# One v tile as a third fp32 load on Scalar's queue, and lambda as one row spread by a PE product

## The chip, the cores and the metric

The kernel runs on one core of a Trainium2 chip. The time is device time in microseconds (us). The kernel before takes 226.63 us (three runs, 226.57 to 226.72).

The profile is one execution. Its engines are PE (TensorE matmul), PEld (TensorE weight loads), DVE (VectorE), ACT (ScalarE), POOL (GpSimd) and SP (SyncE). Its span is about 2 us shorter than the time of the run (224.5 against 226.6). Times inside an execution count from the start of the span. `L238` in a profile line is line 238 of that kernel; the change adds lines, so L238 of before is L247 of after.

## The reference, cut to what matters

A decayed linear attention over 4 batches and 8 heads of 768 positions by 64, and behind it a gated feed-forward layer (512 to 1536 to 512) on its output.

```python
pos = np.arange(block); rel = pos[:, None] - pos[None, :]
Dmask = np.where(rel >= 0, lam[:, None, None] ** rel[None, :, :], 0.0)
...
for b in range(nb):
    intra = np.einsum('bhic,bhjc->bhij', qb, kb) * Dmask[None]
    intra = np.einsum('bhij,bhjd->bhid', intra, vb)
    inter = np.einsum('bhid,bhde->bhie', qb * lam_pow[None], kv_state)
    out[:, :, sl] = intra + inter
    kv_state = lam_block[...] * kv_state + np.einsum('bhsd,bhse->bhde', kb_dec, vb)
...
gate = 1.0 / (1.0 + np.exp(-(x @ w_gate)))
return (gate * (x @ w_val) @ w_out)
```

The kernel takes blocks of 128 positions, six of them. `lam` is eight numbers; each partition needs all of them, for the decay of q (`lamq`) and for the mask.

## The kernel before

Each engine is given its instructions in the order in which the program is written, and where it matters here the traces show it keeping to that order (in h below, PE starts on a k that landed at 7.03 us only at 7.34, behind the transposes of q). The feed-forward products of block n fill PE while the attention of the next block is prepared; block 0 has nothing to hide behind, so its loads and its attention are the head of the kernel.

Three queues of loads feed the head: GpSimd's (`software_dynamic` in part 3 of the page), whose loads go from fp32 to bf16 on the way; Scalar's and Sync's (`hardware_dynamic` there) bring two q tiles as fp32, which are cast on an engine.

```python
lam_bc = const.tile([128, H], FP32, tag="lam_bc")
nc.sync.dma_start(out=lam_bc, in_=lam.partition_broadcast(128))     # 128 x 32 bytes
WG = const.tile([128, NMT, DFF], BF16, tag="WG")                    # and WV, WO
...
q01 = [const.tile([128, H, D], FP32, tag=f"q{b}f", name=f"q{b}f") for b in range(2)]
nc.scalar.dma_start(out=q01[0], in_=q[0, :, 0:C, :].rearrange("h s d -> s h d"))
nc.sync.dma_start(out=q01[1], in_=q[1, :, 0:C, :].rearrange("h s d -> s h d"))
Q[0] = qkv.tile([128, B, H, D], BF16, tag="qb", name="qb")
...
load(0, "k", 0, 2)        # GpSimd's queue, fp32 in DRAM to bf16 in SBUF
load(0, "k", 2, 4)
load(0, "q", 2, 3)
load(0, "q", 3, 4)
load(0, "v", 0, 1)
load(0, "v", 1, 2)
load(0, "v", 2, 3)
load_w(WG, wg_r, 0, GW // 2)
...
idle(10)                  # products of zeros, which keep PE busy
nc.vector.tensor_copy(Q[0][:, 0], q01[0])
piece_tq0([0])            # PE transposes of q, then QS on DVE
make_mask(0)
idle(1)
piece_tq0([1])
piece_tk0(0)              # PE transposes of k ("tk"), then KS copies on ACT
make_mask(1)
idle(1)
piece_s(0, [0])           # scores "sp" = KS x QS
piece_m(0, 0)             # masked scores "MT" on DVE
piece_s(0, [1])
piece_m(0, 1, (0,))
piece_tk0(1)
...
piece_a0(0)               # "op" = MT x v, copied to XT
piece_a0(1)
idle(2)
piece_a0(2, (nc.scalar.copy, nc.scalar.copy))
g0 = psum()
mm_part(g0, WG, 0, 0, 0, 3 * C)      # the first feed-forward product, "gp"
```

A tile pool hands out SBUF one tile after the other (here each started on a multiple of 32 bytes). The pool `const` comes first, `qkv` (the bf16 tiles of q, k and v) right behind it. The built program lists where each tile starts, in bytes within a partition:

```
                before                 after
lam_bc          16512                  16512
lam1                -                  16544   (32 bytes)
WG              16544                  16576
q0f, q1f        53408, 55456           53440, 55488
v0f                 -                  57536   (2048 bytes)
ones                -                  512 bytes, behind zero
first qkv tile  68352 = 534 x 128      70944 = 554 x 128 + 32
```

A load by GpSimd of q, k or v writes each head of a position as one run of 64 bf16 numbers, so 128 bytes (in the trace these loads are packets of 128 bytes). In before each such run starts on a multiple of 128 bytes.

## Time and profile before

| | before |
|---|---|
| time, median (range, runs) | 226.63 us (226.57 to 226.72, 3) |
| span of the profiled run | 224.5 us |
| PE busy | 217.8 us, 97% |
| first k landed | 7.53 us |
| first feed-forward product (gp) starts | 14.51 us |

The page of before, part 1 (busy us, share of the span, instructions) and part 4 (shares of the chain that ended last):

```profile
PE 217.8 (97%) x1746; PEld 114.7 (51%) x1746; DVE 105.8 (47%) x192; ACT 79.8 (36%) x151; POOL 79.2 (35%) x78
...
PE 94%; DMA 3%; ACT 1%; issue 1%; DVE 0%; POOLq 0%
```

PE bounds the kernel; the 3% of DMA on the chain is one load, the first k. The chain of waits of before in the first 15.6 us (start, duration, what):

```profile
1.26 6.26 DMA kb<-in_k_dram
...
7.57 0.41 PE tk L238 x4
...
8.01 1.08 ACT KS L267 x2
...
9.90 0.59 ACT KS L267
...
11.18 0.44 DVE QS L256
...
13.78 0.29 PE op L313 x3
...
14.51 1.14 PE gp L434 x6
```

The first k load is issued at 1.26 us and lands at 7.53; the engines then pass the work on with almost no slack until the first feed-forward product. A microsecond more on k's landing should be a microsecond on the whole.

The view of loads of before in the first 20 us (destination and source, issuing queue, number, KB each, median us from issue to landing):

```profile
kb<-in_k_dram POOLq DMA_DIRECT2D x2, 256.0 KB, 6.5
vb<-in_v_dram POOLq DMA_DIRECT2D x4, 128.0 KB, 6.2
q0f<-in_q_dram ACTq DMA_DIRECT2D x1, 256.0 KB, 4.2
lam_bc<-in_lam_dram SPq DMA_DIRECT2D x1, 4.0 KB, 3.1
```

Lambda's 4 KB take 3.1 us, where the 256 KB of the first q take 4.2.

### The profile page before, as it was taken

How to read it: one execution, taken by the hardware profiler on the slowest of the kernel's cores; microseconds unless marked ns; L12 is line 12 of the kernel's file. 1: busy time of each engine (PE TensorE's matmuls, PEld its weight loads, DVE VectorE, ACT ScalarE, POOL GpSimd, SP SyncE). 2: the span in 40 equal slices, each digit the busy share in tenths (PEclk: the TensorE clock that was granted, in tenths of full speed). 3: DMA queues.
4: the chain of work that ended last, by engine and by line, in shares of the span. 5: the costliest groups of instructions: out<-in, count | busy, mean ns of one | idle time of the engine just before them, and what ended most of it. 6: DMA issues, size and time to landing. Idle time of an engine off the chain costs nothing.

```text
span 224.5 us, 4262 instructions
## 1 busy us (share of the span) xinstructions
PE 217.8 (97%) x1746; PEld 114.7 (51%) x1746; DVE 105.8 (47%) x192; ACT 79.8 (36%) x151; POOL 79.2 (35%) x78
## 2 busy tenths in 40 slices
PE   7689999999999999999999999999999999999994
PEld 2454455888854454444445444446444445444443
DVE  7797747595521713336732445742335840333300
ACT  5564334435422234333225333115333225333221
POOL 8996698983592008930006940000000000000000
PEclk9999999999999999999999999999999999999999
DMA  6999999999999992999021999021930012100022
GB/s 109 155 169 193 191 176 155 163 183 168 157 162 159 225 236 86 210 157 101 1 96 55 231 151 128 0 96 47 168 70 0 0 52 91 47 3 0 0 93 95
DMA packets 106419, 25.70 MB, mean 114 GB/s; under 512 B 97056, under 2 KB 103456, under 8 KB 106400
## 3 DMA queue, kind: packets, MB, share of 16 engines
q0 software_dynamic: 81792, 13.90, 81.6%
q1 hardware_dynamic: 23568, 11.28, 20.4%
q10 hardware_dynamic: 1040, 0.26, 0.5%
q8 instruction: 13, 0.21, 0.4%
q14 instruction: 6, 0.05, 0.1%
HBM read 28.32 MB, written 6.29 MB: 154 GB/s over the span
## 4 chain that ended last, share of the span: by engine, by line
PE 94%; DMA 3%; ACT 1%; issue 1%; DVE 0%; POOLq 0%
PE po L483 27%; PE gp L420 21%; PE vp L426 21%; PE gp L455 5%; PE gp L434 5%; PE vp L461 5%; PE sp L300 3%; PE op L313 3%; DMA kb<-in_k_dram 3%; PE op L325 1%; PE po L472 1%; PE cp L404 1%; ACT KS L267 1%; PE tk L238 1%; ACT XT L352 0%
## 5 line engine op out<-in xcount | busy, mean ns | idle before, releaser
L429 DVE TENSOR_TENSOR ht<-sg,vp 128x512 bf16<-128x512 bf16 x54 | 37.1, 687 | 64.2 <-PE vp L426 64.0
L483 PE MATMUL po<-WO,ht 128*128 128x512 bf16 x276 | 62.0, 379 | 0.0
L420 PE MATMUL gp<-XT,WG 128*128 128x512 bf16 x216 | 55.5, 379 | 0.0
L426 PE MATMUL vp<-XT,WV 128*128 128x512 bf16 x216 | 55.4, 379 | 0.0
L423 ACT ACTIVATE sg<-gp 128x512 bf16<-128x512 f32 x54 | 32.2, 597 | 59.0 <-PE gp L420 59.0
L483 PEld LDWEIGHTS <-ht 128*128 128x128 bf16 x276 | 26.3, 98 | 31.0
L426 PEld LDWEIGHTS <-WV 128*128 128x128 bf16 x216 | 21.2, 98 | 25.5
L420 PEld LDWEIGHTS <-WG 128*128 128x128 bf16 x216 | 20.8, 98 | 24.7
L486 ACT COPY ob<-po 128x512 f32<-128x512 f32 x23 | 13.5, 586 | 52.2 <-PE po L483 50.4
L204 DVE TENSOR_TENSOR MT<-sp,mask 128x512 bf16<-128x512 f32 x40 | 25.1, 682 | 9.1 <-PE sp L300 9.1
L382 POOL TENSOR_TENSOR sd<-Sb,dec 128x512 f32<-128x512 bf16 x8 | 8.1, 1037 | 41.2 <-DVE Sb L411 41.1
L455 PE MATMUL gp<-XT,WG 128*128 128x256 bf16 x96 | 14.4, 273 | 0.0
L461 PE MATMUL vp<-XT,WV 128*128 128x256 bf16 x96 | 14.4, 273 | 0.0
L465 DVE TENSOR_TENSOR ht<-sg,vp 128x256 bf16<-128x256 bf16 x24 | 10.0, 420 | 8.6 <-PE vp L461 8.6
L458 ACT ACTIVATE sg<-gp 128x256 bf16<-128x256 f32 x24 | 9.2, 384 | 13.0 <-PE gp L455 11.8
L91 POOL DMA_DIRECT2D vb<-in_v_dram x10 | 12.7, 1278 | 1.0 <-DMA WG<-in_moe_w_gate_dram 0.6
L373 POOL TENSOR_TENSOR kd<-kb,kds 128x1024 bf16<-128x1024 bf16 x6 | 11.3, 1904 | 4.7 <-PE vp L461 4.7
L411 DVE TENSOR_TENSOR Sb<-cp,sd 128x512 bf16<-128x512 f32 x8 | 5.2, 686 | 15.5 <-PE cp L404 15.5
L340 ACT CAST XT<-op 128x512 bf16<-128x512 f32 x19 | 9.9, 598 | 2.1 <-PE op L313 2.0
L455 PEld LDWEIGHTS <-WG 128*128 128x128 bf16 x96 | 9.2, 98 | 1.7 <-issue 0.2
L461 PEld LDWEIGHTS <-WV 128*128 128x128 bf16 x96 | 9.4, 98 | 1.1
L77 POOL DMA_DIRECT2D qb<-in_q_dram x8 | 9.4, 1182 | 0.0
(79 smaller groups left out, 162.1 us busy)
## 6 DMA issues: line engine op xcount, KB each, us to landing
out_dram<-ob SPq DMA_DIRECT2D x21, 256.0 KB, 2.0
kb<-in_k_dram POOLq DMA_DIRECT2D x10, 256.0 KB, 8.4
qb<-in_q_dram POOLq DMA_DIRECT2D x8, 256.0 KB, 8.1
vb<-in_v_dram POOLq DMA_DIRECT2D x4, 512.0 KB, 13.7
WO<-in_moe_w_out_dram POOLq DMA_DIRECT2D x3, 512.0 KB, 8.7
WV<-in_moe_w_val_dram POOLq DMA_DIRECT2D x5, 256.0 KB, 8.8
WG<-in_moe_w_gate_dram POOLq DMA_DIRECT2D x4, 256.0 KB, 8.6
qb<-in_q_dram POOLq DMA_DIRECT2D x6, 128.0 KB, 8.3
```

The source lines that it names most:

```text
L91: nc.gpsimd.dma_start(out=lst[n][:, b0:b1], in_=src[b0:b1, :, sl, :].rearrange("b h s d -> s (b h) d"))
L204: nc.vector.tensor_tensor(out=out.rearrange("p (e x) c -> p e x c", e=2), in0=x.rearrange("p (e x) c -> p e x c", e=2), in1=mask.rearrange ...
L373: nc.gpsimd.tensor_tensor(out=KD[n][:, e], in0=K[n][:, e], in1=kds[:, e::2].unsqueeze(1).unsqueeze(3).to_broadcast([128, B, HP, D]), op=AL ...
L420: nc.tensor.matmul(gp, lhsT=WG[:, mt, fs], rhs=x[:, mt, :], start=(mt == 0), stop=(mt == NMT - 1))
L423: nc.scalar.activation(sg, gp, AF.Sigmoid)
L426: nc.tensor.matmul(vp, lhsT=WV[:, mt, fs], rhs=x[:, mt, :], start=(mt == 0), stop=(mt == NMT - 1))
L429: nc.vector.tensor_mul(HT[n, ft], sg, vp)
L434: nc.tensor.matmul(ps[:, lo:hi], lhsT=W[:, mt, ft * 128:(ft + 1) * 128], rhs=x[:, mt, lo:hi], start=(mt == 0), stop=(mt == NMT - 1))
L455: nc.tensor.matmul(gp[:, cs], lhsT=WG[:, mt, fs], rhs=x[:, mt, cs], start=(mt == 0), stop=(mt == NMT - 1))
L461: nc.tensor.matmul(vp[:, cs], lhsT=WV[:, mt, fs], rhs=x[:, mt, cs], start=(mt == 0), stop=(mt == NMT - 1))
L483: nc.tensor.matmul(po, lhsT=HT[n, ft][:, tt * 128:(tt + 1) * 128], rhs=WO[:, ft, :], start=(ft == 0), stop=(ft == NFT - 1))
L486: nc.scalar.copy(ob, po)
```

## The change

Two halves. The v half: batch 0's v no longer comes as a load on GpSimd's queue but as a third fp32 load on Scalar's hardware queue, with a cast on ACT; every GpSimd load behind it moves up one place. The lambda half: instead of 128 descriptors of 32 bytes, one row of lambda is loaded and PE spreads it (a row of ones times the row of lambda). The ten idle products are split in four, before that product, and six.

```diff
     lam_bc = const.tile([128, H], FP32, tag="lam_bc")
-    nc.sync.dma_start(out=lam_bc, in_=lam.partition_broadcast(128))
+    lam1 = const.tile([1, H], FP32, tag="lam1")
+    nc.sync.dma_start(out=lam1, in_=lam.partition_broadcast(1))
 ...
     nc.sync.dma_start(out=q01[1], in_=q[1, :, 0:C, :].rearrange("h s d -> s h d"))
+    v0f = const.tile([128, H, D], FP32, tag="v0f")
+    nc.scalar.dma_start(out=v0f, in_=v[0, :, 0:C, :].rearrange("h s d -> s h d"))
 ...
+    V[0] = qkv.tile([128, B, H, D], BF16, tag="vb", name="vb")
 ...
+    ones = const.tile([1, 128], FP32, tag="ones")
+    nc.vector.memset(ones, 1.0)
 ...
-    load(0, "v", 0, 1)
     load(0, "v", 1, 2)
 ...
+    idle(4)
+    lamp = ps_at.tile([128, H], FP32, name="lamp", tag="ps")
+    nc.tensor.matmul(lamp, lhsT=ones, rhs=lam1, start=True, stop=True)
     lnl = const.tile([128, H], FP32, tag="lnl")
-    nc.scalar.activation(lnl, lam_bc, AF.Ln)
+    nc.scalar.activation(lnl, lamp, AF.Ln)
 ...
-        nc.scalar.activation(lnp[us, :], lam_bc[us, u::2], AF.Ln)
+        nc.scalar.activation(lnp[us, :], lamp[us, u::2], AF.Ln)
+    nc.scalar.copy(lam_bc, lamp)
 ...
-        parts = 2 if n == 0 and tt < 2 else 1
+        parts = 2 if n == 0 and tt < 1 else 1
 ...
-    idle(10)
+    idle(6)
 ...
     piece_m(0, 1, (0,))
+    nc.scalar.copy(V[0][:, 0], v0f)
     piece_tk0(1)
```

## The prediction

> **What bounds the kernel.** The page gives PE 217.8 of 224.5 us (97%); the chain of waits is 94% PE. From 16.67 us PE runs nearly without a break (timeline); only the first 16 us can give time. There the chain is: first k load issued 1.26, landed 7.53 us -> transposes -> two KS copies on ACT (8.01-9.08) -> sp -> third KS (9.90) -> fourth -> QS on DVE (11.18) -> sp -> five mask products back to back on DVE (11.85-14.92) -> op of batch 2 (13.78, released by its mask product, not by v) -> XT -> gp (14.51).
>
> **What the change removes.** One GpSimd load. These land 0.85 us apart (10.04, 10.89, 11.75, 12.58, 13.45 us), so each load behind v0 should land about 0.85 us sooner. Few are waited for on the chain: v0 is not (op starts 12.31, v0 landed 11.75); v1 (12.58) costs 0.06 us, hidden by the mask products; v2 and v3 nothing. The only later chain stall on a load is at the block-1 k transposes, 32.29 us: 0.16 us. Gain: about 0.15 us.
>
> **What it moves.** v0 as fp32 (1024 packets of 256 B) goes behind q0 on Scalar's queue. [...] while q1's packets run (4.3-5.3 us), k gets 6 to 79 packets per 0.1 us, afterwards 120. v0 needs some 1.0 us at q's rate. Against that, lambda's broadcast goes: its 128 packets of 32 B drag from 1.7 to 3.5 us, and meanwhile q0 gets 42 packets per 0.1 us, afterwards 75. Estimate: three fp32 loads at 1000 packets per us from 2.1 us end at 5.2 us, where two end at 5.3 now. So the first k should land at 7.5 us, give or take 0.3; this goes one to one into the time.
>
> **What it adds.** A PE product ([...]the idle products keep their number, 10), a lambda copy on ACT (0.2 us, like its neighbours), the v0 cast on ACT (0.62 us, like q1's). The cast falls between the second KS and the third, a gap of 0.82 us: free, if v0 has landed by 9.1; I expect 6. The PE product delays the first q transposes by perhaps 0.3 us (5.79 -> 6.1); they have slack until k lands. The store split once less is neutral.
>
> **Prediction.** 226.63 - 0.15 +- 0.3 (k): 226.5 us, 226.0 to 227.2. Faster by over 2%: 1%; within 2%: 98%; slower: 1%.
>
> **What the profile would show.** First k landing 7.2-7.9 us; lambda near 2.5 instead of 3.82; v0 5.5-6.5; v1 about 11.75; first WG about 13.3; third KS at 9.90 plus k's shift, within 0.3; op 2 still released by DVE; gp start 14.51 within 0.3; the 32.29 stall gone; PE busy after 17 us unchanged.
>
> **What would make it wrong.** (a) v0 delaying the first k by its full 1 us: +0.8 us. (b) The gap in the idle products shifting the time when PE gets its full clock (6.03 us in the trace). [...] (c) v0 landing after 9.1 us, holding KS. (d) Earlier q0 and q1 do not pay: k gates them.

The forecast's sum: 226.63 - 0.15 (the gain) +- 0.3 (k) comes to about 226.5 us.

## More of the kernel before

A kernel is run several times, and the median of the fast runs is given with their range.

Busy time by stretch in before (stretch, its length, busy us and number of instructions of PE, PEld, DVE, ACT and POOL; then PE's granted clock, the DMA share, GB/s):

```profile
5.00:10.00 5.00, 3.71 (x40) 1.84 (x39) 3.61 (x8) 3.16 (x11) 5.00 (x7) 1.00 2.38 157
10.00:15.00 5.00, 3.80 (x58) 2.56 (x58) 4.79 (x10) 4.07 (x7) 4.75 (x7) 1.00 2.24 162
```

The DMA share here is the sum of the packets' times over the engines' time; at 2.38 and 2.24 it is above 1, so packets overlap on an engine.

## The result, and the profile after

After takes 227.41 us (227.34 to 227.43, four runs) against 226.67 (226.57 to 226.72, four runs) of before. The ratio is 1.0033, with a 95% interval of 1.0015 to 1.0050. Here and below a ratio is the mean time of one kernel's fast runs over that of the other's of the same rounds, so not quite the ratio of the medians. The change costs 0.74 us by these medians, where a gain of 0.15 was predicted.

The page of after:

```profile
PE 218.4 (97%) x1748; PEld 115.1 (51%) x1748; DVE 106.3 (47%) x193; ACT 80.3 (36%) x153; POOL 78.3 (35%) x77
...
PE 93%; DMA 3%; ACT 1%; DVE 1%; issue 1%; POOLq 0%
```

The shares say nothing; the chain of waits of after does:

```profile
1.26 7.08 DMA kb<-in_k_dram
...
8.38 0.41 PE tk L247 x4
...
8.81 1.08 ACT KS L276 x2
...
10.71 0.59 ACT KS L276
...
11.99 0.42 DVE QS L265
...
14.70 0.29 PE op L322 x3
...
15.43 0.32 PE gp L443
```

It is the same chain, 0.81 us later from its first link on: k is issued at 1.26 us as before and lands at 8.34 instead of 7.53. The last link, gp, is 0.92 later. Nothing new stands between them. The loads of after:

```profile
kb<-in_k_dram POOLq DMA_DIRECT2D x2, 256.0 KB, 7.3
...
vb<-in_v_dram POOLq DMA_DIRECT2D x3, 128.0 KB, 7.3
q0f<-in_q_dram ACTq DMA_DIRECT2D x1, 256.0 KB, 3.3
...
v0f<-in_v_dram ACTq DMA_DIRECT2D x1, 256.0 KB, 5.3
```

The first q is faster by 0.9 us, which is the lambda half at work. But the loads of k and v take 0.8 to 1.1 us longer, and the v loads do so too although one load fewer stands before them. By stretch, after:

```profile
5.00:10.00 5.00, 3.57 (x31) 1.82 (x31) 2.95 (x8) 2.88 (x10) 4.62 (x6) 1.00 2.62 159
10.00:15.00 5.00, 4.07 (x66) 2.61 (x66) 4.76 (x9) 4.06 (x6) 4.01 (x6) 1.00 2.91 155
```

Here is the clue. From 10 to 15 us the three hardware loads have long landed (the last at 6.53), yet the DMA share is 2.91 instead of 2.24 while the rate is 155 GB/s instead of 162. Packets take longer and bring less: in this stretch a packet of 128 bytes takes 32 ns on average in before and 46 in after. The third load has no packet left by then (its last ended at 6.00 us), so it does not compete for the engines in this stretch.

The packet and semaphore records show where in a load the time lies. Each of these loads closes on every one of the 16 engines with a packet of 4 bytes; then the semaphore counts. "Lag" below is the mean over the 16 engines of the time from the end of that packet to the count.

| load, in order of issue | before: landed, lag | after: landed, lag |
|---|---|---|
| k, batches 0 and 1 | 7.53, 0.30 | 8.34, 0.99 |
| k, batches 2 and 3 | 9.20, 0.32 | 10.15, 1.10 |
| q, batch 2 | 10.04, 0.31 | 11.05, 1.11 |
| q, batch 3 | 10.89, 0.30 | 11.95, 1.11 |
| v, batch 0 | 11.75, 0.30 | (6.53, Scalar's queue) |
| v, batch 1 | 12.58, 0.31 | 12.86, 1.11 |
| WG, first part | 14.19, 0.30 | 14.30, 0.80 |

The last of the 16 closing packets of the first k ends at 7.19 us in before and at 7.41 in after: 0.22 later. The other 0.59 of the 0.81 us lie behind that packet. And q's two loads land 0.85 us apart in before, 0.90 in after.

Two more numbers from the same records show the order of things. From 7.0 to 8.5 us a packet of 128 bytes still takes 32 ns in after, though the first k already has a lag of 0.99; only later do packets stretch, to 49 ns on average from 8.7 to 11.0 us (32 in before). And the weights' loads that follow start with a lag of 0.80 and are down to 0.31 by the fifth of them. Why the lag comes first and the longer packets after it, no run shows.

### The profile page after: what moved, and what is told of

Same layout as the page of the kernel before. It is cut to its first block, busy times and chain, and to the rows that moved or that the text cites. A ratio compares the mean times of both kernels' runs of the same rounds, so it can differ in the third digit from the quotient of the medians.

```text
span 225.3 us, 4270 instructions
## 1 busy us (share of the span) xinstructions
PE 218.4 (97%) x1748; PEld 115.1 (51%) x1748; DVE 106.3 (47%) x193; ACT 80.3 (36%) x153; POOL 78.3 (35%) x77
## 4 chain that ended last, share of the span: by engine, by line
PE 93%; DMA 3%; ACT 1%; DVE 1%; issue 1%; POOLq 0%
PE po L492 27%; PE gp L429 21%; PE vp L435 21%; PE gp L464 5%; PE gp L443 5%; PE vp L470 5%; DMA kb<-in_k_dram 3%; PE sp L309 3%; PE op L322 3%; PE op L334 1%; PE po L481 1%; PE cp L413 1%; ACT KS L276 1%; DVE MT L211 1%; PE tk L247 1%
## 5 line engine op out<-in xcount | busy, mean ns | idle before, releaser
L92 POOL DMA_DIRECT2D vb<-in_v_dram x9 | 12.0, 1332 | 0.7 <-DMA WG<-in_moe_w_gate_dram 0.6
```

Source lines behind the costliest of these rows:

```text
L92: nc.gpsimd.dma_start(out=lst[n][:, b0:b1], in_=src[b0:b1, :, sl, :].rearrange("b h s d -> s (b h) d"))
```

## The experiments

Two theories stood after this.

- **Contention**: the third fp32 load goes ahead of k on the same engines and delays it, as risk (a) of the prediction has it.
- **Place**: the added tiles moved the bf16 tiles off a multiple of 128 bytes, and loads that write in runs of 128 bytes are slower there.

A third, that the PE product or the clock costs the time, was watched on the way. To move tiles, a small unused tile is added to `const`; one memset on DVE much later (before block 1's lambda powers) writes to it. All results are correct. The runs are named below by the first letter of their label, given in each heading.

### d: before, with every tile 32 bytes further

```diff
+    pad = const.tile([128, 8], FP32, tag="pad")
     WG = const.tile([128, NMT, DFF], BF16, tag="WG")
 ...
     keep(1)
+    nc.vector.memset(pad, 0.0)
     lamq_start()
```

> The kernel before, with one unused 32-byte tile per partition behind lambda's: every later tile then starts 32 bytes further on, as in the changed kernel (q, k and v tiles 32 past a multiple of 64, weights and q01 on one). Nothing else moves. Theory 1 (the third fp32 load stands before k on the DMA engines): k lands at 7.5 to 7.7 us, time within 0.2 us of before (226.67). Theory 2 (the 32-byte shift of the tiles makes the k, q and v loads slow): k lands at 8.1 us or later, time 227.2 or more, and the time from a load's last packet to its landing rises from 0.3 to about 1 us.

Measured: 227.48 us (227.12 to 228.33, six runs; before in the same rounds 226.60), ratio 1.0045 (1.0028 to 1.0063). The lag is 0.85 at the first k and 1.06 later; k lands at 7.95 and gp starts at 15.07. In the timeline of PE the transposes of k wait for k as in after:

```profile
8.00 0.62 PE L239 MATMUL tk<-ident,kb 128*128 128x128 bf16 x8 [0.75 <-DMA kb<-in_k_dram]
```

So 32 unused bytes make before slower by as much as the whole change does, with no load and no product added. Place is a cause.

### c: after, with a pad, first try

```diff
+    pad = const.tile([128, 8], FP32, tag="pad")
     WG = const.tile([128, NMT, DFF], BF16, tag="WG")
```

> The changed kernel, with the same unused 32-byte tile, so that all tiles start at the same offset from a multiple of 64 bytes as in the kernel before. Theory 1: k lands at 8.1 to 8.3 us, time 227.2 to 227.4. Theory 2: k lands near 7.6 us, time 226.5 to 226.8.

Measured: 227.45 us (227.08 to 227.62, five runs), ratio 1.0034 (1.0021 to 1.0047); k landed at 8.34, lag 1.01 and 1.12. This looked like a blow to the theory of place, but the pad was chosen badly: I had thought of a multiple of 64 bytes, and the tiles came to lie 64 bytes past a multiple of 128. The run shows that 64 past is as bad as 32 past, and nothing on an aligned after. In its profile PE's clock also fell to half from 8.44 to 11.85 us and held gp to 16.00; more on that under b.

### a: the lambda half alone, with the same pad

The v half of the change is undone and c's pad kept; again the tiles lie 64 bytes past 128, where they were meant to be aligned.

```diff
-    v0f = const.tile([128, H, D], FP32, tag="v0f")
-    nc.scalar.dma_start(out=v0f, in_=v[0, :, 0:C, :].rearrange("h s d -> s h d"))
 ...
+    load(0, "v", 0, 1)
     load(0, "v", 1, 2)
 ...
-        parts = 2 if n == 0 and tt < 1 else 1
+        parts = 2 if n == 0 and tt < 2 else 1
 ...
-    nc.scalar.copy(V[0][:, 0], v0f)
```

> Only the lambda half of the change (one row, PE product, copy), tiles at the offsets of before. Theory 1 and theory 2 both: two fp32 loads start at 1.8 instead of 2.3 us without the broadcast beside them, so they end about 0.5 us sooner and k lands at 7.1 to 7.5 us; time 226.2 to 226.7. Theory 3 (the PE product, not the loads, costs the time, by moving the time when PE gets its full clock from 6.0 to 6.9 us): time 227.0 or more with k landing no later than 7.5 us.

Measured: 226.46 us (226.04 to 227.23, six runs), ratio 0.9995 (0.9979 to 1.0011). k lands at 7.06 with a lag of 0.62, and gp starts at 14.34, earlier than in before. So k's landing gains from the lambda row even with misplaced tiles; what the place costs here shows up at 73.6 us, see "Where the place costs" below.

### b: the v half alone, broadcast kept

```diff
-    lam1 = const.tile([1, H], FP32, tag="lam1")
-    nc.sync.dma_start(out=lam1, in_=lam.partition_broadcast(1))
+    nc.sync.dma_start(out=lam_bc, in_=lam.partition_broadcast(128))
 ...
-    idle(4)
-    lamp = ps_at.tile([128, H], FP32, name="lamp", tag="ps")
-    nc.tensor.matmul(lamp, lhsT=ones, rhs=lam1, start=True, stop=True)
 ...
-    idle(6)
+    idle(10)
```

v0f is 2048 bytes, so the tiles stay on a multiple of 128.

> Only the v half of the change (third fp32 load on Scalar's queue, its cast, one GpSimd load less), lambda by broadcast as before, tiles at the offsets of before. Theory 1: the third load costs k its full time and nothing is won back from the broadcast: k lands at 8.5 to 9.0 us, time 227.5 to 228.0, slower than the full change. Theory 2: k lands at 7.5 to 7.8 us, time within 0.3 us of before.

Measured: 229.76 us (229.47 to 230.36, four runs), ratio 1.0135 (1.0117 to 1.0152). The lag is 0.31, as it should be. k lands at 9.10 us: with lambda's 128 small descriptors still in the way (they run to 4.1 us here, to 3.5 in before), q lands at 5.54 and 6.86, v at 7.83, and k pays for all of them, 1.57 us against before. Contention is real. The second cost is in the timeline of PE (start, length, engine, line, operation, [idle time and what ended it]):

```profile
9.15 1.03 PE L240 MATMUL tk<-ident,kb 128*128 128x128 bf16 x8 [1.19 <-DMA kb<-in_k_dram]
```

These eight transposes took 0.62 us in before and in after. The clock records have the full clock from 5.12 to 8.53 us and then half of it until 18.77; gp starts at 18.13, 3.62 us later than in before. In these records the stretches at one clock are multiples of 3.41 us: here 3.41 at full and 10.24 at half, in before and after 218.45 (64 x 3.41) at full. The clock fell after a stretch of 3.41 us in which PE was still busy for 1.33 us by the trace (0.79 of them in transposes), with idle gaps of 0.60 and 0.90 us before the transposes of q and 1.19 us before those of k. In c it fell to half for 3.41 us after one with 1.59 us; in l (below) it stayed full after one with 1.87 us (5.04 to 8.45). Three such stretches make no rule.

### l: before, with only the tiles from lp on moved by 32 bytes

The pad stands behind the weights and the fp32 tiles, so those keep their places.

```diff
+    padb = const.tile([128, 8], FP32, tag="padb")
     lp = const.tile([128, HP, C], FP32, tag="lp")
```

> The kernel before, with one unused 32-byte tile between the weights and the q, k, v tiles: only the bf16 tiles that are loaded and used start 32 bytes further on (32 past a multiple of 128, where they started on one); weights and the fp32 q tiles stay where they were. The runs so far with these tiles off a multiple of 128 (by 32 or 64) all show 0.6 to 1.1 us from a load's last packet to its landing and 0.90 us per 128 KB load, the two with them on it 0.3 and 0.85. If that place is the cause: as the run with all tiles shifted, k lands near 7.95 us, lag near 1 us, time 227.2 to 227.6. If it is the fp32 tiles or the weights: as before, 7.5 us, 0.3 us, 226.6.

Measured: 227.69 us (227.09 to 228.07, six runs; before in the same rounds 226.64), ratio 1.0044 (1.0031 to 1.0058). Lag 0.83 and 1.04, q's loads 0.90 us apart, k at 7.91. By stretch:

```profile
10.00:15.00 5.00, 3.53 (x57) 2.33 (x57) 4.77 (x10) 4.00 (x7) 4.42 (x6) 1.00 2.85 155
```

A share of 2.85 at 155 GB/s, where before has 2.24 at 162 and after 2.91 at 155. The kernel has the loads of before and the signature of after; its first k loads take longer too (6.5 us in before):

```profile
kb<-in_k_dram POOLq DMA_DIRECT2D x2, 256.0 KB, 6.9
```

The place of the weights and of the fp32 tiles is not needed for it. The weights' loads lag here too, by 0.81 us at first, although their tiles did not move, so it seems to come from the loads before them. One limit: every tile behind the pad moves, also those that only engines use. The engines' steps on the chain don't show it, though: the first four transposes of k take 0.41 us and the two KS copies 1.08 in before, after and f alike, and what is slow is in the records of the loads.

### f: after, with q, k and v back on a multiple of 128

```diff
+    padb = const.tile([128, 120], FP32, tag="padb")      # 480 bytes: 70944 + 480 = 558 x 128
     lp = const.tile([128, HP, C], FP32, tag="lp")
```

> The changed kernel, with an unused tile that puts the q, k and v tiles at the offset of before (256 past a multiple of 512). The run with the 32-byte tile had left them 64 past a multiple of 128. Theory 1 (the loads ahead of k): k still lands late, at 7.9 us, since 0.42 us of its 0.81 were the tiles' place; lag back to 0.3, 0.85 us per load; time 226.8 to 227.1. Theory 2 (the place alone): k at 7.5, time 226.5. If the place does not matter here: 8.34 us and 227.4 again.

Measured: 226.18 us (226.08 to 226.40, five runs; before 226.64), ratio 0.9981 (0.9968 to 0.9994). The chain of waits, the loads and the stretch:

```profile
1.26 6.24 DMA kb<-in_k_dram
...
9.87 0.59 ACT KS L277
...
14.48 1.14 PE gp L444 x6
```

```profile
kb<-in_k_dram POOLq DMA_DIRECT2D x2, 256.0 KB, 6.5
vb<-in_v_dram POOLq DMA_DIRECT2D x3, 128.0 KB, 6.3
```

```profile
10.00:15.00 5.00, 3.60 (x57) 2.57 (x58) 4.79 (x10) 4.04 (x7) 4.72 (x7) 1.00 2.17 165
```

This is the pair that decides, although the two were not run in the same rounds (before took 226.67 beside after and 226.64 beside f). The same program with 480 unused bytes is 1.2 us faster than after and a little faster than before. Not all of that lies in what the profile covers. Time minus span is 2.1 to 2.2 us in every run of before, after, d, b, l and m, and 1.7 to 1.9 in every run of c, a, f, h, k, j, i and n; why, no trace shows. So kernels of the two groups are better compared by their spans: by the medians of these f is 0.9 us faster than after (224.4 against 225.25) and 0.1 faster than before (224.5).

Lag 0.30, loads 0.83 to 0.85 us apart, k at 7.50, v of batch 1 at 11.73, the first WG at 13.31, gp at 14.48: nearly every number of the prediction, which was right about a kernel with the tiles of before (in part by luck, see below).

### h: the lambda half alone, aligned

f without the v half (undone as in a).

> Lambda half alone, with the q, k and v tiles at the offset of before. With them 64 past a multiple of 128 k landed at 7.06 and the time was 226.46. If the lambda row and the place add up: k at 6.6 to 6.8 us, lag 0.3, third-to-last q load at 10.2; time 225.8 to 226.1, faster than both kernels.

Measured: 225.97 us (225.59 to 226.29, six runs), ratio 0.9971 (0.9959 to 0.9982). k lands at 7.03 us, 0.47 earlier than in f, and gp starts at 14.27. So with the lambda row in place the third load does delay k by 0.47 us, but it costs only 0.2 us of gp and of time: in h the transposes of k start at 7.34 and not at 7.03, because the transposes of q stand before them in the program and PE is still at those. In the timeline of PE:

```profile
6.92 0.58 PE L246 MATMUL tq<-ident,qb 128*128 128x128 bf16 x4
7.34 0.61 PE L246 MATMUL tk<-ident,kb 128*128 128x128 bf16 x8
```

### k: the first k, not v, as the third fp32 load, on top of h

```diff
-    load(0, "k", 0, 2)
+    load(0, "k", 1, 2)
 ...
+    k0f = const.tile([128, H, D], FP32, tag="k0f")
+    nc.scalar.dma_start(out=k0f, in_=k[0, :, 0:C, :].rearrange("h s d -> s h d"))
 ...
+    nc.scalar.copy(K[0][:, 0], k0f)
```

> The lambda half, aligned tiles, and as third fp32 load on Scalar's queue the first k instead of the first v; the GpSimd load of k is halved. The third load then carries what the chain waits for: k's first half lands near 6.3 us, its second near 6.8 (7.50 with v in its place). Theory 1 (order of the bytes ahead of k): transposes start at 7.1 to 7.3, time 225.7 to 226.1, against 226.18 with v there. If the third load itself delays the rest of the stream instead, the later k and q loads land no sooner than with v and the time is 226.2 or more.

Measured: 225.92 us (225.63 to 226.33, six runs), ratio 0.9969 (0.9952 to 0.9986): the same as h. k0f lands at 6.64 and the other half at 7.13, so the chip has k no earlier than h has.

### j, m, i: where the place of the other tiles matters

Three runs ask this: j, before with the weights and the fp32 q tiles on a multiple of 512 (88 and 40 fp32 numbers of padding), m, before with the tiles from lp on moved by 128 bytes, and i, the lambda half with all of these aligned.

```diff
+    pada = const.tile([128, 88], FP32, tag="pada")       # j; 80 in i
     WG = const.tile([128, NMT, DFF], BF16, tag="WG")
 ...
+    padb = const.tile([128, 40], FP32, tag="padb")       # j and i; 32, without pada, in m
     lp = const.tile([128, HP, C], FP32, tag="lp")
```

> The kernel before with weights and fp32 q tiles on a multiple of 512 (they stood 32 past a multiple of 128), q, k and v tiles unmoved. If a place off 128 costs the fp32 loads as it costs the bf16 ones, q0 and q1 land 0.1 to 0.3 us sooner and k with them: 7.3 us, time 226.3 to 226.5. If it matters for the 128-byte runs alone: as before, 226.6.

> The kernel before, with the q, k and v tiles 128 bytes further on: still on a multiple of 128, no more on one of 256. If 128 bytes is the size that counts (each of these loads writes runs of 128 bytes): as before, k lands near 7.5 us, lag 0.3, 0.85 us per load, 226.6 us. If any move of the tiles costs, or 256 is the size: lag near 1 us, 0.90 us per load, k at 7.9, 227.4.

> Lambda half alone, with q, k, v tiles on a multiple of 256 and also weights and fp32 q tiles on one of 512 (64 past 128 in the run before this). k's landing was 7.03 there, but its transposes began at 7.34, held by PE's own order. So even if q0, q1 and k land 0.2 us sooner the time should not follow: 225.8 to 226.2.

Measured: j 226.58 us (ratio 0.9992, 0.9980 to 1.0004), m 226.66 (1.0003, 0.9984 to 1.0023), i 226.11 (0.9980, 0.9965 to 0.9995). In time none is told apart from its partner (before, before, h); by the medians of the spans j is 0.3 us longer than before (224.8 against 224.5).

- m: 128 bytes more do no harm; the lag is 0.30. Since a tile's runs of 128 bytes lie one behind the other, half of them start 128 past a multiple of 256 in before too, so this run can't tell a boundary of 128 from one of 256.
- The fp32 loads seem to gain from a better place: q lands at 4.72 and 5.61 in j, at 4.92 and 5.99 in before, and k at 7.29. The gain is given back at 18.52 us, where PE waits 0.56 us for a WV load that lands at 18.47 (17.25 in before). Why that load is late stays open.
- The weight loads write runs of 256 bytes. They lie 32 bytes past 128 in before already, with a lag of 0.30, and the first WG and WV land 0.72 us apart; in j, on a multiple of 512, 0.76, with lags of 0.30 and 0.33. These runs show no harm to runs of 256 bytes.

### n: h with two idle products fewer

In h PE's order held k. So one of six idle products is taken away, and the one between the two transposes of q.

```diff
-    idle(6)
+    idle(5)
 ...
-    idle(1)
     piece_tq0([1])
```

> Lambda half alone, aligned tiles, and two of the idle PE products in front of the k transposes left out (the profile had q transposes, idle product and second q transposes end only at 7.3 us, after k's landing at 7.03). If PE's order holds the chain: k transposes at 7.1, chain 0.2 us sooner, 225.6 to 225.9. If the masks on DVE hold it (they end 8.77, just before the first masked product at 8.84), only what the q transposes win, 0.1 us. If PE loses its clock for lack of work: 226.5 or more.

Measured: 225.81 us (225.74 to 225.86, five runs), ratio 0.9963 (0.9950 to 0.9976). PE keeps its full clock (1.00 from 5 to 15 us). The chain of waits begins with the load again:

```profile
1.26 5.99 DMA kb<-in_k_dram
...
7.29 0.41 PE tk L246 x4
...
14.24 1.46 PE gp L442 x8
```

In the profiled runs this gains 0.03 us of gp over h, with k landing later here (7.25 against 7.03); in time the two are not told apart (225.97, range 225.59 to 226.29). It is faster than before and after, and has the lowest median, though h and k are not told apart from it.

### Where the place costs

With the first k, gp and any later wait, the span of each profiled run can be added up from before's 224.5 us. One later wait is in before itself, 0.17 us at 32.28 us for block 1's k, in the timeline of PEld:

```profile
32.28 0.22 PEld L281 LDWEIGHTS <-kb 128*128 128x128 bf16 x4 [0.17 <-DMA kb<-in_k_dram]
```

| kernel | q, k, v past 128 | first k landed | gp starts | later wait of PE for a load | span |
|---|---|---|---|---|---|
| before | 0 | 7.53 | 14.51 | 0.17 at 32.28 | 224.5 |
| after | 32 | 8.34 | 15.43 | none | 225.3 |
| d, before shifted | 32 | 7.95 | 15.07 | 0.26 at 74.03 | 225.2 |
| l, before from lp on | 32 | 7.91 | 15.04 | 0.73 at 74.47 | 225.7 |
| c, after, first pad | 64 | 8.34 | 16.00 | none | 225.8 |
| a, lambda half | 64 | 7.06 | 14.34 | 0.57 at 73.61 | 224.8 |
| b, v half | 0 | 9.10 | 18.13 | none | 228.3 |
| f, after aligned | 0 | 7.50 | 14.48 | none | 224.3 |
| h, lambda half | 0 | 7.03 | 14.27 | none | 224.1 |
| j, before, all aligned | 0 | 7.29 | 14.27 | 0.56 at 18.52 | 224.8 |
| m, before + 128 | 0 | 7.33 | 14.32 | 0.34 at 32.30 | 224.5 |
| i, lambda half, all aligned | 0 | 7.16 | 14.15 | 0.21 at 31.97 | 224.2 |
| k, k as third load | 0 | 7.13 | 14.45 | none | 224.3 |
| n, fewer idle | 0 | 7.25 | 14.24 | none | 224.0 |

For after: 224.5 + 0.92 (gp) - 0.17 (the wait gone) = 225.25; measured 225.3. For f: 224.5 - 0.03 - 0.17 = 224.3; measured 224.3. For l: 224.5 + 0.53 - 0.17 + 0.73 = 225.6; measured 225.7. For n: 224.5 - 0.27 - 0.17 = 224.06; measured 224.0. For i: 224.5 - 0.36 - 0.17 + 0.21 = 224.18; measured 224.2. In b the sum is 0.3 short, where the clock is still at half after gp begins (to 18.77 us); in j it is 0.2 short (224.65 against 224.8), which stays open.

The wait at 74 us is a second cost of the place, which the runs d, l and a have on the chain. In the timeline of PE in l:

```profile
74.47 0.62 PE L301 MATMUL sp<-QS,KR 64*128 64x128 bf16 x16 [0.73 <-DMA KR<-kb]
```

KR is block 2's k, transposed by DMA after its load. Block 2's two k loads land 1.81 us apart in l and in after, 1.66 in before and 1.67 in f. In after itself PE comes to this point later (74.06 against 73.31 in before) and KR, landed at 73.58, is just in time. So l's slowdown is not of the same make-up as after's, although the cause is; it would be wrong to read the 0.53 us of gp as the price of the place in every kernel.

## Why the prediction was wrong

The prediction was 226.5 us with a range of 226.0 to 227.2; measured were 227.41. Point by point:

- **The failing step is "What it moves"**, where the first k "should land at 7.5 us, give or take 0.3". It landed at 8.34. The step counted packets in the queues and took for granted that the loads themselves stay as fast as before. I never looked at where the tiles lie. The change adds 32 + 512 + 2048 bytes to the pool in front of q, k and v, which shifts them by 2592 = 20 x 128 + 32 bytes. Off a multiple of 128 (32 and 64 past were tried), q, k and v loads landed 0.90 us apart instead of 0.85, with a lag of 1.0 to 1.1 us in after instead of 0.30 (0.6 to 1.1 over the other misplaced kernels). With 480 bytes of padding the same program had k at 7.50 and took 226.18 us. The cause, that is the place of these tiles, is shown from both sides: before shifted has the signature of after (l), after shifted back has that of before (f).
- **Risk (a), v0 delaying k by about 1 us, was not what happened**, though +0.8 us was the size that came. f has the same third load and k on time. The chip did show the risk without the lambda row: 1.57 us in b. In the company of the lambda row the third load delays k by 0.47 us (h to f).
- **The rate of the hardware loads was mis-sized.** The estimate was 1000 packets per us, ending at 5.2 us. Measured in after: 3072 packets from 1.83 to 6.00 us, so about 740 per us (830 in f), and v landed at 6.53, just past the predicted 5.5 to 6.5. That k was on time in f all the same is because two terms happened to cancel: the lambda row alone brings k from 7.53 to 7.03 us (before to h), the third load takes it back to 7.50 (h to f). The prediction put both near 1 us; that the difference was right is in part luck.
- **Loads on different queues do hold each other up**, as the prediction read from the packet counts of before: after has v0's packets at 25 ns each where the first q's took 18, and b shows the price in full (k 1.57 us later).
- **The cast on ACT** was right: it fits into the gap between the second and the third KS. In the timeline of ACT in after:

```profile
9.91 0.62 ACT L521 CAST vb<-v0f 128x512 bf16<-128x512 f32 x1
10.71 0.58 ACT L276 COPY KS<-tk 128x512 bf16<-128x512 bf16 x1 [0.17 <-PE tk L247]
```

- **The PE product** took 0.59 us from 3.01 in after (two PE instructions in the trace) and was free in after and f, since it stands among idle products ahead of the wait for k. In h it is not: there PE's own order is the chain from the start, with 0.52 us of this product on it. Lambda landed at about 1.9 us (its one packet at 1.6); 2.5 was predicted.
- **The gain** was right in size: the wait of 0.17 us at 32.28 is gone, and the span grew by 0.8 while gp slipped by 0.92. That the removed load is what gave it is not shown: the wait is gone in h too, where no load was removed (block 1's second k load lands at 32.24 in before, 31.33 in f, 31.09 in h).
- **v of batch 1 and the first WG** were predicted for 11.75 and 13.3 and came at 12.86 and 14.30 in after, at 11.73 and 13.31 in f. It is the same failing step again.
- **Risk (b), the clock**, did not strike after: full from 6.86 us, the eight transposes of k in 0.62 us as in before. It struck b and the profiled run of c, and one run of d has a mean clock of 0.985 and the longest time of d (228.33).
- **op of batch 2 released by DVE, PE unchanged after 17 us**: right. In after's chain the link ahead of op is a mask product on DVE, and from 20 us to 40 PE is busy 20.00 us in both.

What stays open is the mechanism under the place. The sources of the loads are the same in all kernels; between before and l only the place of the tiles from lp on differs (and one memset much later). How the chip handles a run of 128 bytes that does not start on a multiple of 128 no run shows. Two things that an explanation would have to fit: 32 past and 64 past are alike (lag 0.99 and 1.11 us in after, 1.01 and 1.12 in c), and the weights' runs of 256 bytes at 32 past 128 show no added lag (0.30 in before).

## What to carry to other kernels

A change that adds or removes tiles also moves every tile behind them; compare the start addresses before and after, and try the targets of loads that write runs of 128 bytes on a multiple of 128. Off it, such loads cost this kernel some 0.8 to 1.1 us of its span in the three pairs that show it (medians: d 225.3 and l 225.55 against before 224.5, after 225.25 against f 224.4). A broadcast of a few bytes can cost the loads beside it, too: here the first q load got 42 packets per 0.1 us while 128 packets of 32 bytes ran and 75 afterwards (75 at once in after, from 2.4 to 3.4 us), and taking them away made the first k land 0.5 us earlier (7.53 to 7.03). When loads that the change does not touch get slower, look at the DMA share against GB/s in a stretch where the added load has already ended: here the share rose from 2.24 to 2.91 while the rate fell from 162 to 155 GB/s, from 10 to 15 us, when the added load's last packet had ended at 6.00, and it was the layout. An unused tile, one in the old kernel and one in the new, tests the layout from both sides.
